# Attention and two experts on one core: reciprocal row sums spread by a GpSimd copy and five transposes instead of 64-column matmuls, and q/k transposes over all 128 rows

## The chip, the cores and the metric

The kernel runs on one core of one Trainium2 chip. The metric is the device time of one execution in microseconds; lower is better. The kernel uses five engines, each with its own instruction queue that is worked off in order: TensorE (PE, its weight loads shown as PEld), VectorE (DVE), ScalarE (ACT), GpSimd (POOL) and SyncE (SP), which issues the DMAs.

## What is computed

Attention over 2 batches and 8 heads of 576 rows and 64 columns, its output rearranged to 1152 tokens of 512, and two experts after it.

```python
def _attn_ref(q, k, v):
    ...
    q_rot, k_rot = (rotate(q), rotate(k))
    scale = 1.0 / np.sqrt(D)
    scores = scale * np.matmul(q_rot, k_rot.transpose(0, 1, 3, 2))
    scores = scores - np.max(scores, axis=-1, keepdims=True)
    attn = np.exp(scores)
    attn = attn / (np.sum(attn, axis=-1, keepdims=True) + 1e-09)
    return np.matmul(attn, v).astype(np.float32)

def reference(**kwargs):
    ...
    x = np.ascontiguousarray(attn_out.transpose(0, 2, 1, 3)).reshape(B * S, H * D)
    x = _moe_ref(x=x, **moe_kwargs)
    return _moe2_ref(x=x, **moe2_kwargs)
```

`_moe_ref` is `((x w_a) * (x w_b)) w_out` with 1536 inner columns, `_moe2_ref` is `(h - tanh(h)) w_out` with `h = x w_in` and 2048 inner columns.

## The kernel before

The attention works on eight pairs of heads, numbered 0 to 7. The 576 rows of a head are held as 64 rows by 9 chunks, two heads side by side: chunks 0 to 4 of a tensor stand on partitions 0 to 63 and chunks 5 to 8 on partitions 64 to 127, so that four columns of blocks (`c` = 0 to 3) fill 128 partitions and the fifth (`CM`, chunk 4) fills 64; its other 64 partitions were set to zero at the start.

For each pair the steps are:
- `load_qk`, `rope_step` (rope, on DVE for pair 1 and on POOL from pair 2 on, tiles `r2` and `ro`), `prep_T`: the rotated tensor is transposed by TensorE into `psp` (line 362), split by ACT and DVE into two parts and spread by DMA. Pair 0 goes through `rope_head` and `prep_head` (line 323) instead.
- `s_unit` (nine a pair): scores into `pss` (line 408, four matmuls), the negated maximum on DVE (line 414); `s_exp`: the exponential on ACT with the row sums in `sm` (line 420).
- `t_unit` and `t_tail`: the exponentials are transposed into `pst` (lines 473, 454, 459, 460), then split by ACT (478) and DVE (480) into `ph`.
- `v_head`: four accumulations over `ph` with v into `acc` (line 500), copied by ACT into `xe`; for pairs 0 to 6 one half goes by DMA into `xsum` (line 524) and POOL adds the other (line 525, two adds a pair); the last pair does it on DVE.
- `norm_sum`: 1 / (sum + 1e-9) into `rs`, 128 partitions by 9.
- `norm_pair`: the nine columns of `rs` have to stand along the free axis on 64 partitions each. A plain matmul with the column, broadcast to 64 columns, as the weights and the identity as the moving operand does it: eight of 128 columns into `rb` (line 557), two of 64 into `rt` (line 561), each into one half of the partitions. DVE multiplies `xsum` by `rb` (569) and `rt` (571), casts it to `xt` (577), and POOL subtracts for the low part (578).

`rb`, `rt`, `psp` and `pst` share the pool `ps_t`, tag `t`, with three buffers; `pss` has two. `norm_pair` already had a second way, with a tile `rd` in which `norm_sum` spreads `rs` to 128 columns for each of five blocks:

```python
rd = ap1.tile([P, 5, P], F32, tag="rd", name="rd")
fn = (nc.vector.tensor_copy, nc.gpsimd.tensor_copy, nc.scalar.copy)[RDP]
```

`ap1` has one buffer per tag. The number `RDP` in the table `CFG` chooses: 3 the matmuls, 1 the copy on POOL.

The order is set in two stages. A table of events places each step at a multiple of half a unit (nine units a pair): `at(g0 + NS, norm_sum, j)`, `at(t0 - 18 + NP, norm_pair, j)`, with `NS` 19 and `NP` 31, so that a pair's `norm_pair` comes ten units after its `norm_sum` and one unit after the `norm_sum` of the next pair. A scheduler then orders the instructions on each engine by priorities and by its own view of readiness and adds the waits. The expert stages follow: ACT and DVE convert the weights in pieces while TensorE multiplies (lines 190 and 843).

Of the kernel before, what the change touches and what calls it, by code (L numbers as in the profile page):

```python
# [29 lines left out]
def attention_moe_kernel(  # L30
# [184 lines left out]
    # ------------------------------------------------------------ attention  # L215
    with ExitStack() as actx:
# [703 lines left out]
```

## Time and profile before

| | us |
|---|---|
| median of 3 runs | 632.19 |
| lowest and highest | 631.37, 632.22 |
| span of the profiled execution | 632.1 |
| PE busy in it | 608.2 |
| DVE, ACT, POOL busy | 481.1, 348.4, 132.4 |

The profile is of one execution, whose span of 632.1 us agrees with the median. Busy time of PE contains the overlap of matmuls that follow each other: an instruction's own duration is longer than the distance to the next one's start. How long a step holds TensorE is therefore read from starts. A group of rows names the line, engine, operation, tile written and tiles read; in the timeline a row merges neighbours of one kind (x4), and square brackets show an idle time before it and who ended it. `128*64` is rows by columns of the array in use, `128x128` what is moved.

### The profile page before, as it was taken

What the parts mean: (1) busy time and instruction counts of PE and PEld (TensorE: products, weight loads), DVE (VectorE), ACT (ScalarE), POOL (GpSimd) and SP (SyncE); (2) the same over time, 40 slices, a digit from 0 to 9 for tenths busy, and PEclk for the clock granted to TensorE, in tenths of its full rate; (3) what the DMA queues carried; (4) which work ended last, traced back from release to release, by engine and by line L of the source; (5) the groups of instructions that cost most, each with busy time, mean ns of one, the idle gap of its engine ahead of it and who ended that gap; (6) DMA issues with size and microseconds to landing.
All of it is one profiled execution on the core that took longest, in us unless ns stands there. A gap on an engine that the chain in (4) does not pass through costs nothing.

```text
span 632.1 us, 9300 instructions
## 1 busy us (share of the span) xinstructions
PE 608.2 (96%) x3588; PEld 568.3 (90%) x3588; DVE 481.1 (76%) x646; ACT 348.4 (55%) x579; POOL 132.4 (21%) x121
## 2 busy tenths in 40 slices
PE   7789999999999999999999999998999999999997
PEld 6578988998889999999999999988988988998975
DVE  6868877778788988787757568694976698899572
ACT  2468877787774555533323133356966673585350
POOL 4565877773331000000000000091000000000000
PEclk7789999999999999999999999997999999999999
DMA  3466656753542555534203123320001121310014
GB/s 85 124 157 150 141 131 152 174 127 92 140 153 67 171 166 185 167 111 130 71 8 126 67 67 133 107 94 1 1 1 66 67 66 41 100 60 1 1 40 110
DMA packets 37771, 60.92 MB, mean 96 GB/s; under 512 B 4064, under 2 KB 22496, under 8 KB 37728
## 3 DMA queue, kind: packets, MB, share of 16 engines
q1 hardware_dynamic: 37728, 60.34, 33.3%
q8 instruction: 28, 0.46, 0.3%
q14 instruction: 15, 0.12, 0.1%
HBM read 43.06 MB, written 2.36 MB: 72 GB/s over the span
## 4 chain that ended last, share of the span: by engine, by line
PE 79%; DVE 6%; ACT 6%; POOL 3%; DMA 3%; issue 2%; SPq 1%; POOLq 0%; ACTq 0%; DVEq 0%
PE ab L190 24%; PE h L190 11%; PE o L843 10%; PE y L190 9%; PE acc L500 6%; PE pss L408 6%; PE pst L473 4%; POOL yt L736 3%; PE ow L843 3%; PE psp L362 2%; PE rb L557 2%; ACT st L127 1%; DMA st<-in_moe_w_in_dram 1%; DMA st<-in_moe_w_out_dram 1%; DVE nm L414 1%
## 5 line engine op out<-in xcount | busy, mean ns | idle before, releaser
L190 PE MATMUL ab<-xt,w 128*128 128x384 f32 x504 | 88.6, 334 | 0.5 <-ACT w L152 0.5
L190 PEld LDWEIGHTS ab<-xt,w 128*128 128x128 f32 x504 | 87.4, 188 | 0.8 <-ACT w L152 0.8
L843 PE MATMUL o<-wc,g 128*128 128x512 f32 x348 | 83.8, 392 | 0.4 <-ACT g L818 0.3
L843 PEld LDWEIGHTS o<-wc,g 128*128 128x128 f32 x348 | 64.7, 188 | 14.1 <-ACT g L818 1.3
L190 PE MATMUL y<-g,wc 128*128 128x384 f32 x432 | 76.5, 334 | 0.0
L190 PEld LDWEIGHTS y<-g,wc 128*128 128x128 f32 x432 | 75.0, 188 | 0.0
L408 PE MATMUL pss<-k,q 128*128 128x288 f32 x320 | 64.7, 323 | 2.4 <-ACT p L420 1.3
L414 DVE TENSOR_REDUCE nm<-pss 128x1 f32<-128x576 f32 x72 | 54.0, 753 | 15.9 <-PE pss L408 15.6
L190 PE MATMUL h<-yt,w 128*128 128x384 f32 x360 | 65.4, 335 | 0.1
L190 PEld LDWEIGHTS h<-yt,w 128*128 128x128 f32 x360 | 62.9, 188 | 1.7 <-issue 0.5
L736 POOL TENSOR_TENSOR yt<-yacc,yt 128x384 fp32r<-128x384 f32 x12 | 19.8, 1685 | 207.4 <-ACT yt L735 207.4
L190 PE MATMUL ab<-xt,wc 128*128 128x384 f32 x360 | 63.2, 334 | 0.0
L190 PEld LDWEIGHTS ab<-xt,wc 128*128 128x128 f32 x360 | 62.5, 188 | 0.0
L127 ACT ACTIVATE st<-st 128x1024 f32<-128x1024 f32 x34 | 39.9, 1172 | 35.5 <-DMA st<-in_moe_w_b_dram 16.2
L420 ACT ACTIVATE p<-pss,nm 128x576 f32<-128x576 f32 x72 | 54.0, 750 | 6.6 <-DVE nm L414 6.3
L500 PE MATMUL acc<-ph,v 128*128 128x288 f32 x320 | 55.4, 305 | 0.9 <-ACT ph L478 0.9
L408 PEld LDWEIGHTS pss<-k,q 128*128 128x128 f32 x320 | 47.5, 196 | 7.0 <-ACT p L420 4.3
L480 DVE TENSOR_TENSOR ph<-pst,ph 128x512 fp32r<-128x512 f32 x72 | 48.4, 684 | 4.8 <-ACT ph L478 4.6
L703 ACT COPY tmpa<-ab 128x384 f32<-128x384 f32 x36 | 17.2, 478 | 61.9 <-PE ab L190 61.7
L478 ACT CAST ph<-pst 128x512 fp32r<-128x512 f32 x72 | 42.4, 595 | 10.9 <-PE pst L473 9.5
L500 PEld LDWEIGHTS acc<-ph,v 128*128 128x128 f32 x320 | 45.1, 188 | 2.0 <-issue 1.5
L473 PE MATMUL pst<-ident,p 128*128 128x128 f32 x288 | 45.5, 276 | 1.0 <-DVE ph L480 1.0
(118 smaller groups left out, 1009.1 us busy)
## 6 DMA issues: line engine op xcount, KB each, us to landing
st<-in_moe_w_out_dram SPq DMA_DIRECT2D x14, 1024.0 KB, 4.9
st<-in_moe_w_in_dram SPq DMA_DIRECT2D x8, 1024.0 KB, 5.2
q<-th SPq DMA_DIRECT2D x28, 288.0 KB, 4.9
st<-in_moe_w_a_dram SPq DMA_DIRECT2D x12, 512.0 KB, 3.8
st<-in_moe_w_b_dram SPq DMA_DIRECT2D x12, 512.0 KB, 5.0
k<-th SPq DMA_DIRECT2D x28, 160.0 KB, 2.7
vr<-in_v_dram SPq DMA_DIRECT2D x16, 128.0 KB, 2.9
out_dram<-oacc SPq DMA_DIRECT2D x16, 128.0 KB, 2.4
```

The costliest lines, as they stand in the source:

```text
L127: nc.scalar.activation(out=xs.bitcast(F32), in_=xs.bitcast(F32), func=AF.Copy, scale=2.0 ** -112)
L190: nc.tensor.matmul(ps, w(a), x(c), start=start and n == 0, stop=stop and n == 2)
L408: nc.tensor.matmul(ph[:, a], st, k2[i][:, j, ko + a * HS:ko + (a + 1) * HS], start=(n == 0), stop=(n == len(mms) - 1),)
L414: nc.vector.tensor_reduce(out=nm[:, u:u + 1], in_=ph, axis=AX.XY, op=ALU.max, negate=True)
L420: nc.scalar.activation(out=po.rearrange("p (a x) -> p a x", a=2), in_=ph, func=AF.Exp, bias=nm, scale=1.0, accum_out=sm,)
L473: nc.tensor.transpose(ps[:, t * P:(t + 1) * P], p[:, t, o:o + P], ident)
L478: nc.scalar.copy(out=pu[:, 0, qm(i)], in_=ps)
L480: nc.vector.tensor_tensor(out=pu[:, 1, qm(i)], in0=ps, in1=pu[:, 0, qm(i)], op=ALU.subtract)
L500: nc.tensor.matmul(acc, st, pslot(i, u)[:, s, a * HS:(a + 1) * HS], start=(u == 8 and s == 0), stop=(u == full[-1] and s == 1),)
L703: nc.scalar.copy(out=a[:, t], in_=r[0])
L736: (nc.gpsimd if YLP > d else nc.vector).tensor_tensor(out=yl, in0=o, in1=yh, op=ALU.subtract)
L843: nc.tensor.matmul(ps, g[:, a, i * P:(i + 1) * P], wc[:, c, f % 2], start=(n == 0 and m == 0), stop=(n == GE - 1 and m == 2),)
```

## The change

Three things. `RDP` in `CFG` goes from 3 to 1, so `norm_sum` now copies `rs` on POOL into `rd` (512 columns and 128), and `norm_pair` transposes the five blocks of `rd` (four into `rb`, one into `rt`); the product with `rt` becomes two of 64 partitions. In `prep_T` the `CM` block is transposed over all 128 rows, and the next block overwrites the 64 columns too many or nothing reads them. In `prep_head` the same holds for the first head (`j` = 0). Four section comments and one on a formula go too. With the old way's branches gone the line numbers move: 408 becomes 409, 473 474, 500 501, 525 526, 557 554, 561 555, 362 363; 541 and 545 are the two copies.

```diff
@@ -320,7 +320,8 @@
             w = o = 448 * j
             for c in ((0, 1, 2, 3, CM), (CM, 0, 1, 2, 3))[j]:
                 x = 64 if c == CM else P
-                nc.tensor.transpose(ps[:, w:w + x], src[0:x, c], ident[0:x, 0:x])
+                r = x if j else P
+                nc.tensor.transpose(ps[:, w:w + r], src[0:r, c], ident[0:r, 0:r])
                 w += x
             ps = ps[:, o:w]
             if n == 1:
@@ -359,7 +360,7 @@
             for c in cols:
                 r = 64 if c == CM else P
                 with hp('pT'):
-                    nc.tensor.transpose(ps[:, w:w + r], src[0:r, c], ident[0:r, 0:r])
+                    nc.tensor.transpose(ps[:, w:w + P], src[:, c], ident)
                 w += r
             with hp('th'):
                 nc.scalar.activation(out=th[:, o:o + w], in_=ps[:, 0:w], func=AF.Copy, scale=sc)
@@ -549,30 +550,14 @@
             rd = rds.pop(i)
             rb = ps_t.tile([P, 512], F32, tag="t", name="rb")
             rt = ps_t.tile([P, 512], F32, tag="t", name="rt")
-            if RDP == 3:
-                for j in range(2):
-                    r = slice(64 * j, 64 * j + 64)
-                    for t in range(CM):
-                        u = 4 * j + t
-                        nc.tensor.matmul(
-                            rb[r, t * P:(t + 1) * P], rd[:, u:u + 1].to_broadcast([P, 64]), ident,
-                            start=True, stop=True,
-                        )
-                    nc.tensor.matmul(
-                        rt[r, 0:64], rd[:, 8:9].to_broadcast([P, 64]), ident[:, r], start=True, stop=True,
-                    )
-            else:
-                for t in range(CM):
-                    nc.tensor.transpose(rb[:, t * P:(t + 1) * P], rd[:, t], ident)
-                nc.tensor.transpose(rt[:, 0:P], rd[:, CM], ident)
+            for t in range(CM):
+                nc.tensor.transpose(rb[:, t * P:(t + 1) * P], rd[:, t], ident)
+            nc.tensor.transpose(rt[:, 0:P], rd[:, CM], ident)
             x = xs_t.pop(i)
             nc.vector.tensor_tensor(out=x[:, qm(i)], in0=x[:, qm(i)], in1=rb, op=ALU.mult)
-            if RDP == 3:
-                nc.vector.tensor_tensor(out=x[:, qt(i)], in0=x[:, qt(i)], in1=rt[:, 0:64], op=ALU.mult)
-            else:
-                for j in range(2):
-                    r = slice(64 * j, 64 * j + 64)
-                    nc.vector.tensor_tensor(out=x[r, qt(i)], in0=x[r, qt(i)], in1=rt[r, r], op=ALU.mult)
+            for j in range(2):
+                r = slice(64 * j, 64 * j + 64)
+                nc.vector.tensor_tensor(out=x[r, qt(i)], in0=x[r, qt(i)], in1=rt[r, r], op=ALU.mult)
             xh, xl = (t[:, hp, b * S:(b + 1) * S] for t in xt)
             (nc.scalar.copy, nc.gpsimd.tensor_copy, nc.vector.tensor_copy)[XHE](out=xh, in_=x)
             nc.gpsimd.tensor_tensor(out=xl, in0=x, in1=xh, op=ALU.subtract)
```

The scheduler's order moves with it. On POOL, where the two adds of pair 2 stand between the v preparation and the k rope of pair 6, the queue before:

```order
L290 TENSOR_TENSOR v_95<-vr,v_95 128x4x64 [waits PE_49,Activation_49,Pool_49]
L525 TENSOR_TENSOR xsum<-xe,xsum 64x576 [waits DMAHW5_49]
L525 TENSOR_TENSOR xsum<-xe,xsum 64x576 [waits DMAHW6_49,Pool_49]
L273 TENSOR_TENSOR r_1497<-rawk,rtab 128x10x32 [waits DMAHW7_49,DMAHW0_49,Pool_49]
L273 TENSOR_TENSOR r_1497<-rawk,rtab 128x10x32
L278 TENSOR_TENSOR ro<-rawk,rtab 128x640 [waits PE_49]
```

and now, the copies for pair 3 reading `rs`:

```order
L290 TENSOR_TENSOR v_95<-vr,v_95 128x4x64 [waits PE_49,Activation_49,Pool_49]
L526 TENSOR_TENSOR xsum<-xe,xsum 64x576 [waits DMAHW5_49]
L541 COPY rd<-rs 128x512 [waits PE_49]
L545 COPY rd<-rs 128x128
L526 TENSOR_TENSOR xsum<-xe,xsum 64x576 [waits DMAHW6_49,Pool_49]
L273 TENSOR_TENSOR r_1497<-rawk,rtab 128x10x32 [waits DMAHW7_49,DMAHW0_49,Pool_49]
L273 TENSOR_TENSOR r_1497<-rawk,rtab 128x10x32
```

The two adds stood together and the k rope followed at once. Now the copies of the next pair stand between them, and the first copy waits for PE, whose transposes of pair 2 read the one buffer of `rd`.

On PE, at the reciprocal step of pair 2, before:

```order
L408 MATMUL pss<-k_1044,q_93 128x288 x4
L557 MATMUL rb<-ident,rs 64x128 x2
L408 MATMUL pss<-k_1044,q_93 128x288 x4
L557 MATMUL rb<-ident,rs 64x128 x2
L561 MATMUL rt<-ident,rs 64x64
L557 MATMUL rb<-ident,rs 64x128 x4
L561 MATMUL rt<-ident,rs 64x64
L500 MATMUL acc<-ph,v_96 128x288
L362 MATMUL psp<-ident,ro 128x64
L362 MATMUL psp<-ident,ro 128x128 x3
L408 MATMUL pss<-k_1044,q_93 128x288 x4
```

and now:

```order
L409 MATMUL pss<-k_1045,q_93 128x288 x4
L554 MATMUL rb<-ident,rd 128x128 x2
L409 MATMUL pss<-k_1045,q_93 128x288 x4
L554 MATMUL rb<-ident,rd 128x128 x2
L555 MATMUL rt<-ident,rd 128x128
L501 MATMUL acc<-ph,v_96 128x288
L409 MATMUL pss<-k_1045,q_93 128x288 x4
L363 MATMUL psp<-ident,ro 128x128 x4
L501 MATMUL acc<-ph,v_96 128x288 x3
L474 MATMUL pst<-ident,p 128x128 x2
```

Ten matmuls of 64 output rows became five transposes, and the k transposes are all of one shape. Between `rt` and the next `pst` there are four `pss`, four `psp` and four `acc` matmuls.

## Rows read from the trace of the kernel before

**Rows 1.** The page: busy time by engine, and the chain by line.

```profile
PE 608.2 (96%) x3588; PEld 568.3 (90%) x3588; DVE 481.1 (76%) x646; ACT 348.4 (55%) x579; POOL 132.4 (21%) x121
PE ab L190 24%; PE h L190 11%; PE o L843 10%; PE y L190 9%; PE acc L500 6%; PE pss L408 6%; PE pst L473 4%; POOL yt L736 3%; PE ow L843 3%; PE psp L362 2%; PE rb L557 2%; ACT st L127 1%; DMA st<-in_moe_w_in_dram 1%; DMA st<-in_moe_w_out_dram 1%; DVE nm L414 1%
```

**Rows 2.** Stretches, one pair each: length, busy by engine, PEclk, DMA share, GB/s.

```profile
102.70:123.10 20.40, 20.11 (x154) 18.48 (x154) 16.03 (x31) 16.30 (x43) 15.30 (x16) 1.00 0.63 150
...
143.50:163.40 19.90, 19.49 (x150) 17.88 (x150) 15.56 (x30) 15.82 (x42) 6.75 (x8) 1.00 0.54 124
```

**Rows 3.** Chain of waits by line, in 62.2 to 143.5, 143.5 to 195, 20 to 62.2.

```profile
by line: PE acc L500 27.2%; PE pss L408 24.5%; PE pst L473 16.8%; PE psp L362 9.8%; PE rb L557 8.7%; DVE ph L447 2.8%; DVE nm L414 2.5%; ACT v L289 1.5%; ACT xe L522 1.5%; issue 1.1%; ACT ph L445 1.0%; PE rt L561 1.0%; PE pst L459 0.5%; PE 
...
by line: PE acc L500 26.4%; PE pss L408 16.8%; PE pst L473 14.2%; PE rb L557 13.3%; ACT p L420 4.6%; PE psp L362 3.9%; ACT st L127 2.3%; ACT w L152 2.2%; DVE st L135 2.2%; issue 2.2%; ACT ph L478 2.1%; PE ab L190 1.9%; DVE ph L447 1.7%; ACT
...
by line: PE pss L408 22.9%; PE acc L500 12.6%; PE pst L473 10.8%; PE psp L362 10.7%; DVE ro L280 8.4%; DVE nm L414 6.2%; ACT p L420 5.2%; DVE ph L480 4.5%; DVE rs L533 3.5%; ACT ph L478 2.8%; issue 2.0%; ACT th L365 1.8%; DVE q L339 1.8%; D
```

**Rows 4.** Groups of PE instructions: xcount | busy us, mean ns | idle before, releaser.

```profile
L473 PE MATMUL pst<-ident,p 128*128 128x128 f32 x288 | 45.5, 276 | 1.0 <-DVE ph L480 1.0
...
L557 PE MATMUL rb<-ident,rs 128*64 128x128 f32 x128 | 14.9, 280 | 2.5 <-DVE ph L447 1.6 <-DVE ph L480 0.9
...
L362 PE MATMUL psp<-ident,ro 64*128 64x64 f32 x28 | 7.8, 278 | 3.7 <-DVE ro L280 2.8 <-DVE ph L480 1.0
```

**Rows 5.** PE in order of time, 102 to 112: start us, us, instruction.

```profile
102.75 0.62 PE L557 MATMUL rb<-ident,rs 128*64 128x128 f32 x4 [0.38 <-DVE ph L447]
103.30 0.78 PE L408 MATMUL pss<-k,q 128*128 128x288 f32 x4
104.01 0.71 PE L557 MATMUL rb<-ident,rs 128*64 128x128 f32 x6
...
105.42 0.40 PE L500 MATMUL acc<-ph,v 128*128 128x288 f32 x1
105.75 0.75 PE L362 MATMUL psp<-ident,ro 64*128 64x64 f32 x4
106.25 0.77 PE L408 MATMUL pss<-k,q 128*128 128x288 f32 x4
106.86 0.70 PE L500 MATMUL acc<-ph,v 128*128 128x288 f32 x4
107.39 0.27 PE L473 MATMUL pst<-ident,p 128*128 128x128 f32 x1
...
110.20 1.06 PE L362 MATMUL psp<-ident,ro 64*128 64x64 f32 x6
111.19 0.67 PE L408 MATMUL pss<-k,q 128*128 128x288 f32 x3
```

**Rows 6.** PE in order of time, 187 to 190: eight full transposes.

```profile
187.21 1.04 PE L473 MATMUL pst<-ident,p 128*128 128x128 f32 x8
188.00 1.31 PE L500 MATMUL acc<-ph,v 128*128 128x288 f32 x8
```

**Rows 7.** Groups of POOL instructions: the nearest prices for a copy.

```profile
masks.py:199 POOL TENSOR_SCALAR_AFFINE_SELECT ident<-ident 128x128 f32<-128x128 f32 x1 | 0.3, 292 | 0.1
masks.py:197 POOL MEMSET ident<- 128x128 f32 x1 | 0.2, 205 | 0.3 <-POOLq L898 0.3
...
L898 POOL MEMSET const-float32-0.0<- 128x1 f32 x1 | 0.1, 98 | 0.2 <-issue 0.2
```

**Rows 8.** POOL in order of time, 102 to 124: its longest waits in one pair.

```profile
103.89 1.40 POOL L525 TENSOR_TENSOR xsum<-xe,xsum 64x576 f32<-64x576 f32 x1 [0.70 <-DMA xsum<-xe]
...
108.06 1.56 POOL L278 TENSOR_TENSOR ro<-rawk,rtab 128x640 f32<-128x640 f32 x1 [1.00 <-PE psp L362]
...
120.26 0.32 POOL L296 TENSOR_TENSOR v<-vt,v 64x64 fp32r<-64x64 f32 x1 [1.95 <-ACT v L295]
```

**Rows 9.** DVE in order of time, 122 to 129: the product and its wait.

```profile
125.89 0.69 DVE L569 TENSOR_TENSOR xsum<-xsum,rb 128x512 f32<-128x512 f32 x1 [0.41 <-PE rb L557]
126.49 0.21 DVE L571 TENSOR_TENSOR xsum<-xsum,rt 128x64 f32<-128x64 f32 x1
```

More of the change, by code (lines that the diff above doesn't have):

```diff
@@ L1 @@
-CFG = {'EXPF': 1, 'MAXF': 1, 'TT0': 20, 'TT1': 17.5, 'NS': 19, 'NP': 31, 'LK': -8, 'LQ': -2, 'RK': -2, 'RQ': 1, 'PK': 2, 'PQ': 4.5, 'LV': 7, 'PV': 9, 'WC1': 6, 'WC2': 4, 'PST': 3, 'RE': 2, 'FST': 0, 'CY': 1, 'CA': 2, 'CH': 2, 'OE': 3, 'VA0': 5.5, 'VA1': 7, 'VB0': 0, 'VB1': 2, 'PKD': 1, 'PQD': 0, 'PVD': 2, 'PVE': 0, 'XHE': 2, 'RST': 0, 'PA': 99, 'PB': 0, 'PO': 4, 'YLP': 4, 'GA': 0, 'GB': 0, 'WF': 99, 'WCE': 5, 'NH': 2, 'HA': 0, 'NT2': 2, 'RB': -50, 'SB': -49, 'NW': 20, 'NW1': 6, 'TM': 1, 'CO': 1, 'CHB': 0, 'WG': 99, 'WCG': 4, 'TL': 7, 'P_pl': 0, 'P_norm_sum': 30, 'P_load_v': 0, 'P_prep_v': 30, 'P_pT': 60, 'P_tl': -15, 'XL': 7, 'RDP': 3, 'P_ph': 0, 'P_exp': -60, 'P_V': 0, 'P_rope_head1': 0, 'P_load_qk': 15, 'P_S': 0, 'P_xs': -15, 'P_T': 0}
+CFG = {'EXPF': 1, 'MAXF': 1, 'TT0': 20, 'TT1': 17.5, 'NS': 19, 'NP': 31, 'LK': -8, 'LQ': -2, 'RK': -2, 'RQ': 1, 'PK': 2, 'PQ': 4.5, 'LV': 7, 'PV': 9, 'WC1': 6, 'WC2': 4, 'PST': 3, 'RE': 2, 'FST': 0, 'CY': 1, 'CA': 2, 'CH': 2, 'OE': 3, 'VA0': 5.5, 'VA1': 7, 'VB0': 0, 'VB1': 2, 'PKD': 1, 'PQD': 0, 'PVD': 2, 'PVE': 0, 'XHE': 2, 'RST': 0, 'PA': 99, 'PB': 0, 'PO': 4, 'YLP': 4, 'GA': 0, 'GB': 0, 'WF': 99, 'WCE': 5, 'NH': 2, 'HA': 0, 'NT2': 2, 'RB': -50, 'SB': -49, 'NW': 20, 'NW1': 6, 'TM': 1, 'CO': 1, 'CHB': 0, 'WG': 99, 'WCG': 4, 'TL': 7, 'P_pl': 0, 'P_norm_sum': 30, 'P_load_v': 0, 'P_prep_v': 30, 'P_pT': 60, 'P_tl': -15, 'XL': 7, 'RDP': 1, 'P_ph': 0, 'P_exp': -60, 'P_V': 0, 'P_rope_head1': 0, 'P_load_qk': 15, 'P_S': 0, 'P_xs': -15, 'P_T': 0}
 from contextlib import ExitStack, nullcontext
```

## The prediction

> **What bounds the kernel now.** I read the page's first and fourth parts, then the stretches pair by pair, then the chain of waits in three stretches, then the TensorE rows of one pair. The page says that PE is busy 96% of 632.1 us and heads the chain; lines 362 and 557, which the change touches, are 2% of it each [rows 1]. That is an average over two very different stages. Everything the change touches lies in the attention stage, which ends near 195 us. There one pair of heads, counted from one first `rb` to the next, takes 20.4 us and a later one 19.9. In the former PE is busy for 20.1 us, but DVE (16.0), ACT (16.3) and POOL (15.3) are not far behind, and after 143 us POOL falls to 6.75 because no rope is left [rows 2]. PE's granted clock is 1.00 in these stretches.
>
> A busy PE may still be a waiting PE, since matmuls overlap, so the chain decides. From 62.2 to 143.5 us the five PE lines it names first (500, 408, 473, 362, 557) carry 87% of it, and `rb` (8.7%), `rt` (1.0%) and `psp` (9.8%) together 19.5%. In 143.5 to 195 `rb` is 13.3% and `psp` 3.9%; in 20 to 62.2 `psp` is 10.7%, and DVE and ACT hold much of the rest [rows 3]. So four steady pairs are limited mainly by PE, and these two steps are a fifth of what limits them.
>
> **TensorE, reciprocal sums.** A plain matmul leaves two records, 128 of `rb` for its 64 matmuls over eight pairs, so a pair's ten leave twenty. A transpose leaves one: 288 records of line 473 for 8 x 9 x 4 transposes [rows 4]. In one pair the first four `rb` records hold PE from 102.75 to 103.30 (0.55 us), and the other twelve with four `rt` from 104.01 to 105.42 (1.41 us): 1.96 us [rows 5]. Eight full transposes take 187.21 to 188.00, so 0.099 us each [rows 6]. Five are 0.50 us. A pair saves 1.46 us.
>
> The Trainium skill (TensorEngine Tiling (Array Packing), Key Properties) says that tiles work independently and run in parallel, which speaks against this change: by it half-width matmuls would share the array, the twenty would be worth about 0.98 us, an estimate of half of what the rows show, and the saving a third of mine. The trace does not agree for these: sixteen records in 1.41 us are 0.09 us each, nearly a full transpose's 0.099.
>
> **TensorE, q/k transposes.** Each of seven pairs has two tensors of six transposes; the two 64-row ones become full ones. The q tensor's six hold PE from 110.20 to 111.19, 0.99 us, where six full ones are 0.59; the k tensor's first four hold it from 105.75 to 106.25, 0.50 us, where four are 0.40 [rows 5]. So changing the array's shape costs more than the extra rows. I take 0.4 us for q and 0.3 for k, whose last two also change shape once, plus an entry: one `acc` matmul before the first 64-row transpose takes 0.33 us (105.42 to 105.75), where four in a row take 0.53 (106.86 to 107.39) [rows 5], so 0.2 at an entry. About 1.1 us a pair with two entries.
>
> **PE sum, by the chain.** I count only what the chain holds. 62.2 to 143.5: 19.5% of 81.3 is 15.9 us; in its place stand four times 0.50 and 48 transposes at 0.099, 6.8 us; it saves 9.1. 143.5 to 195: `rb` and `psp` are 17.2% of 51.5, 8.9 us, against four times 0.50 and twelve transposes, 3.2; it saves 5.7. 20 to 62.2: `psp` is 4.5 us against 24 transposes, 2.4; it saves 2.1. Together 16.9 us. Per step without the chain it would be 8 x 1.46 + 7 x 1.1 = 19.4, the most I could defend. The first pair's `prep_head` also widens two transposes from 64 rows to 128; they stand beside DVE's rope and I cost them at nothing, at 2 x 0.099 us if that cover is gone.
>
> **POOL.** New are two copies a pair, 512 and 128 columns. No such broadcast copy is in the trace. From below: a memset takes 98 ns for one column and 205 for 128, 0.84 ns a column, so 0.73 us for the two. From above: the two-input add takes 1.40 us for 576 columns, so 1.56. I take the affine select, which reads one input and writes one output as a copy does: 292 ns for 128 columns, 1.53 ns a column, 1.17 us [rows 7]. That is 9.4 us of POOL over eight pairs. In the ropes' pairs POOL then has 15.3 + 1.2 = 16.5 us of work. In such a pair it is idle for 20.4 - 15.3 = 5.1 us, its longest waits 0.70, 1.00 and 1.95 us [rows 8], which the copy may fill.
>
> The Trainium skill (GPSIMD Engine Reference, section 4.1) has one-input work at roughly line rate. By the 1.03 cycles an element of its section 3.1 the copies would be some 0.55 us, an estimate; the sum below would gain about 1 us. No run here shows it.
>
> **The wait that takes the removed one's place.** `rd` has one buffer, so a pair's copy waits until the transposes of the pair before have read it. The order puts the copies of pairs 3 to 6 (of 0 to 7) between the two adds of the pair before. There the second add, then the DVE product and then the release of `rb` and `rt` all follow the transposes, and these two hold two of the three buffers of `ps_t`. Before, the product waited only for PE, 0.41 us, with both adds done [rows 8, 9]. Now from `rt` to the freed buffer it is 1.17 + 1.40 + 0.69 = 3.26 us. For pair 2 PE has between `rt` and its next `pst` one `acc`, four `pss`, four `psp`, three `acc`: eight matmuls at 0.13 and four transposes, 1.46 us, so about 1.8 us of waiting. For pair 3 it has four `psp`, eight `acc` and four `pss`: 2.0 us, so 1.3. For pair 4 the order has put 3 us of work there, and from pair 5 on no rope competes for the third buffer. I give back 3.1 us. Queued behind the product on DVE are the next maxima, and for those `pss` and ACT's exponentials.
>
> **DVE.** One 128x64 product of 0.21 us becomes two of 64x64, each no longer [rows 9]: 0.2 us a pair, beside 4 us of idle DVE time, at nothing. If DVE becomes the bound it costs 1.7 us in all.
>
> **Haircut and sum.** With a pair at some 18.1 us (20.4 less 9.1/4) DVE and ACT are 90% busy and POOL 91%, all in strict order, so short waits grow. I take a tenth of the saving, 1.7 us; that share is chosen, between nothing and the 8 us of the third case below. 632.1 - 16.9 + 3.1 + 1.7 = 620.0. The span is 632.1 us and the median of the three runs 632.19, so nothing is added. The expert stages have the same work in the same order; I leave them as they are. SP's queue gets no new transfer.
>
> **The rivals.**
> 1. Main case, 616.5 to 624: as above. Chance 0.50.
> 2. PE saving in full: the copy is as cheap as its lower bound, 0.73 us, and the third buffer comes free early. 632.1 - 16.9 = 615.2, 612.7 by the step count; taken as 612.5 to 616.5. For it speaks the chain, against it the 80% loads of DVE and ACT. Chance 0.14.
> 3. POOL or DVE takes over in the four rope pairs, which stay near 20.4 us, and only the 5.7 and 2.1 us outside them are won: 632.1 - 7.8 = 624.3; up to 629 if the tail, where ACT's and DVE's weight parts stand in the chain [rows 3], gives half of its 5.7 back and DVE's 1.7 come on top. For it: POOL's waits are ordered waits and may not be filled by the copy. Chance 0.23.
> 4. No change, within 0.2% (1.3 us, about what a measurement of this kernel can tell from none): PE merely waits where it worked. Against it: 87% of the chain is PE. Chance 0.05.
> 5. Slower: POOL's copy holds up the ropes. A rope pair is then POOL's own: 15.3 of work, 1.6 of copy, the 5.1 us of idle time kept, and 2 us, chosen, of waiting for the transposes: 24.0 us. Four such pairs add 14.4, less 7.8 elsewhere: 638.7. It decides once a rope pair goes above 20.4 + 7.8/4 = 22.4 us. Against it: PE's waits before `psp` name only ropes made on DVE, never POOL's [rows 4]. Chance 0.08.
>
> Could the change fail to do what it says? The order shows five transposes and no 64-row `psp` on PE, so no.
>
> **How the numbers follow.** Cases 1 to 3 are faster: 0.87; case 4 same: 0.05; case 5 slower: 0.08. The likeliest is case 1, 620.0. Its own range is 616.5 to 624. The range to give takes in most of case 2 and of case 3: 613 to 629; outside are cases 4 and 5 and thin ends, some 0.17.
>
> **What would show it.** Right: the profile after has 40 records of `rb` and `rt` in place of 160, all `psp` as 128x128, pairs of about 18 us between one `rb` and the next, a copy row on POOL near 0.9 us for 512 columns, and a `xsum` product that waits for POOL in pairs 2 and 3. Expert stages start some 12 us earlier and last as long. Wrong: pairs still of 20 us with PE idle before `pst` or `pss` (case 3 or 4), PE waiting for `ro` from POOL (case 5), or a lower PE clock in the attention stage, which would upset every price here.

## The result, and the profile after

The changed kernel takes 621.1 us (median of four, 619.34 to 626.83), the kernel before on the same chip 631.78 (628.22 to 632.22). The ratio is 0.986 (0.9818 to 0.9903), so the change wins about 9 us by it, with medians 10.7 apart; 620.0 was forecast, and the range of 613 to 629 holds the result. The total came out nearly as forecast. Where it came from did not, and most of this section is about that.

The page of the changed kernel: busy time by engine, the granted clock in 40 slices, the chain by engine and by line.

```profile
PE 587.5 (95%) x3468; PEld 551.8 (89%) x3468; DVE 486.0 (79%) x654; ACT 347.8 (56%) x579; POOL 133.1 (22%) x137
...
PEclk9999999999999999999999999999999999999999
...
PE 72%; DVE 10%; ACT 8%; POOL 3%; DMA 3%; issue 2%; SPq 0%; POOLq 0%; ACTq 0%; DVEq 0%
PE ab L190 23%; PE h L190 11%; PE o L828 11%; PE y L190 9%; PE pss L409 5%; PE acc L501 5%; PE pst L474 4%; PE ow L828 3%; POOL yt L721 2%; ACT p L421 2%; ACT ph L479 2%; PE psp L363 1%; ACT st L127 1%; POOL xsum L526 1%; DMA st<-in_moe_w_in_dram 1%
```

The chain by engine of the kernel before:

```profile
PE 79%; DVE 6%; ACT 6%; POOL 3%; DMA 3%; issue 2%; SPq 1%; POOLq 0%; ACTq 0%; DVEq 0%
```

Against [rows 1], PE is busy 20.7 us less, and its share of the chain has gone from 79% to 72%, to DVE and ACT; `rb` is gone from the list of lines and POOL's add, line 526, has come in. The span is 617.6 us, that execution's own time 619.34. So a time is some 1.8 us above its span, and the profiled execution of before, span 632.1, must have taken about 633.9.

I split each span at three marks that PE's rows give: the first `rb`, the first `y` matmul, the first `h` matmul. Each row below has a stretch, its length, then busy time and instructions of PE, PEld, DVE, ACT and POOL, then the granted clock, DMA share, GB/s. First the kernel before, in a view not shown ahead:

```profile
0.00:62.20 62.20, 50.23 (x289) 42.88 (x289) 46.64 (x94) 33.70 (x85) 32.74 (x35) 0.84 0.51 127
62.20:231.80 169.60, 165.98 (x1212) 155.63 (x1213) 138.72 (x233) 122.58 (x280) 79.90 (x75) 1.00 0.52 136
231.80:419.00 187.20, 187.20 (x1082) 187.20 (x1081) 135.27 (x172) 74.32 (x97) 9.66 (x7) 1.00 0.32 107
419.00:632.10 213.10, 204.81 (x1010) 182.55 (x1008) 160.50 (x150) 117.78 (x119) 10.13 (x6) 0.98 0.15 46
```

The same of the changed kernel:

```profile
0.00:54.90 54.90, 44.77 (x288) 38.83 (x289) 45.91 (x94) 33.48 (x85) 30.94 (x37) 1.00 0.57 143
54.90:222.00 167.10, 153.89 (x1094) 145.66 (x1093) 142.22 (x241) 121.73 (x279) 84.54 (x89) 1.00 0.52 138
222.00:409.20 187.20, 187.20 (x1082) 187.20 (x1081) 135.73 (x171) 74.19 (x95) 9.47 (x7) 1.00 0.32 107
409.20:617.60 208.40, 201.67 (x1010) 180.11 (x1008) 162.12 (x152) 118.38 (x120) 8.11 (x6) 1.00 0.16 47
```

The 14.5 us between these two spans are 7.3 before the first `rb`, 2.5 from there to `y`, none to `h`, and 4.7 after it. Two things are mixed in them. One is the clock: in the profiled execution of before PE ran at the lower level (1.2 GHz) for 20.5 us ahead of the first `rb` and for 6.8 near 430 us, in that of the change nowhere. These stretches differ between executions of one kernel, and the listed mean clocks show it: 0.977 to 0.993 for 23 executions of before on one chip, 0.984 to 1.000 for four of the change. So the clock is a rival for the whole gain. The times show how much of it: on that chip a straight line through time against listed mean clock falls by 0.32 us for each 0.001, both for the 23 of before and for six of the changed kernel (run e4 below, 0.978 to 0.999). At 0.985 the two lines read 631.1 and 624.6 us. By this estimate some 6.5 us of the gain stand at equal clock, and the other 2 or so come with the higher clocks that the changed kernel's executions had.

The other is the second row: PE's busy time fell by 12.1 us (165.98 to 153.89), but its idle time rose from 3.6 to 13.2 us, so 9.6 of the 12.1 were given back. That row is what the experiments are about.

Groups of the changed kernel: what the new work costs (xcount, then busy us and mean ns of one, then idle time before them and what ended it).

```profile
L363 PE MATMUL psp<-ident,ro 128*128 128x128 f32 x84 | 13.1, 276 | 0.8 <-DVE xsum L560 0.7
...
L562 DVE CAST xt<-xsum 128x576 fp32r<-128x576 f32 x8 | 5.9, 739 | 0.2
L554 PE MATMUL rb<-ident,rd 128*128 128x128 f32 x32 | 5.5, 274 | 0.8 <-DVE ph L481 0.4 <-DVE ph L448 0.4
L557 DVE TENSOR_TENSOR xsum<-xsum,rb 128x512 f32<-128x512 f32 x8 | 5.5, 685 | 4.4 <-POOL xsum L526 4.3
...
L541 POOL COPY rd<-rs 128x512 f32<-128x512 f32 x8 | 4.9, 613 | 9.2 <-PE rt L555 8.0 <-DVE rs L535 1.1
```

All 84 `psp` have the full shape, `rb` has 32 records. POOL waited 8.0 us for the transposes (`rt`) before copies, and DVE 4.3 us for POOL's add before products.

Now pair by pair, from one first `rb` to the next (columns as above), pairs 1, 2 and 3 of 0 to 7:

```profile
75.00:93.10 18.10, 17.46 (x139) 16.90 (x137) 15.36 (x31) 15.39 (x41) 16.07 (x17) 1.00 0.67 161
93.10:114.00 20.90, 18.19 (x136) 16.75 (x137) 17.10 (x32) 16.52 (x43) 18.67 (x20) 1.00 0.62 155
114.00:135.10 21.10, 18.06 (x140) 17.00 (x140) 17.11 (x31) 15.83 (x42) 15.04 (x16) 1.00 0.53 125
```

Pair 1 takes 18.1 us against 20.4 [rows 2], the length forecast for all four. Pairs 2 and 3, the two in which the prediction put the new wait, are longer than before. Pair 0, from 54.9 to 75.0 us, has won nothing either: 20.0 us, before 20.2. PE's waits in pair 2 (in total, times, longest):

```profile
PE pst L474 <- DVE xsum L557: 1.0, 1, 1.0
PE acc L501 <- ACT ph L479: 0.7, 1, 0.7
PE pst L474 <- DVE th L368: 0.6, 1, 0.6
PE rb L554 <- DVE ph L448: 0.4, 1, 0.4
PE pss L409 <- ACT p L421: 0.2, 1, 0.2
```

In pair 1 they are 0.3 us in all, here 2.9, and in pair 3 3.7: nearly the whole difference. POOL in order of time at the start of pair 2 (start us, us, instruction, idle before it):

```profile
92.08 1.42 POOL L526 TENSOR_TENSOR xsum<-xe,xsum 64x576 f32<-64x576 f32 x1
94.86 0.61 POOL L541 COPY rd<-rs 128x512 f32<-128x512 f32 x1 [1.36 <-PE rt L555]
95.41 0.30 POOL L545 COPY rd<-rs 128x128 f32<-128x128 f32 x1
95.79 1.40 POOL L526 TENSOR_TENSOR xsum<-xe,xsum 64x576 f32<-64x576 f32 x1
```

And DVE just behind:

```profile
97.22 0.69 DVE L557 TENSOR_TENSOR xsum<-xsum,rb 128x512 f32<-128x512 f32 x1 [1.25 <-POOL xsum L526]
```

The copy of the next pair stands between the two adds, is released by the transposes, and pushes the second add; the product is late, the bank it should free is late, and PE waits for it before `pst`. That is the mechanism as forecast. Behind it stands something that wasn't: the DVE cast of line 562 (577 before). The kernel before:

```profile
107.73 0.45 DVE L577 CAST xt<-xsum 128x576 fp32r<-128x576 f32 x1
```

In pair 3 of the changed kernel, on DVE:

```profile
120.02 1.78 DVE L562 CAST xt<-xsum 128x576 fp32r<-128x576 f32 x1
121.72 0.61 DVE L368 SCALAR_TENSOR_TENSOR th<-psp,th 128x448 fp32r<-128x448 f32 x1
```

and on POOL at the same time:

```profile
119.93 1.55 POOL L278 TENSOR_TENSOR ro<-rawk,rtab 128x640 f32<-128x640 f32 x1
```

A cast of 0.45 us lasts until 121.80, 0.3 us past the end of POOL's instruction, and `th`, for which PE's `pst` waits, stands behind it. In before the cast began at 107.73, ahead of POOL's rope at 108.06 [rows 8], and was not held: what holds it is the POOL instruction already running when it begins.

### The profile page after: what moved, and what is told of

Same layout as the page of the kernel before. It is cut to its first block, busy times and chain, and to the rows that moved or that the text cites. A ratio compares the mean times of both kernels' runs of the same rounds, so it can differ in the third digit from the quotient of the medians.

```text
span 617.6 us, 9091 instructions
## 1 busy us (share of the span) xinstructions
PE 587.5 (95%) x3468; PEld 551.8 (89%) x3468; DVE 486.0 (79%) x654; ACT 347.8 (56%) x579; POOL 133.1 (22%) x137
## 4 chain that ended last, share of the span: by engine, by line
PE 72%; DVE 10%; ACT 8%; POOL 3%; DMA 3%; issue 2%; SPq 0%; POOLq 0%; ACTq 0%; DVEq 0%
PE ab L190 23%; PE h L190 11%; PE o L828 11%; PE y L190 9%; PE pss L409 5%; PE acc L501 5%; PE pst L474 4%; PE ow L828 3%; POOL yt L721 2%; ACT p L421 2%; ACT ph L479 2%; PE psp L363 1%; ACT st L127 1%; POOL xsum L526 1%; DMA st<-in_moe_w_in_dram 1%
## 5 line engine op out<-in xcount | busy, mean ns | idle before, releaser
L409 PE MATMUL pss<-k,q 128*128 128x288 f32 x320 | 62.4, 315 | 6.6 <-ACT p L421 4.5
L415 DVE TENSOR_REDUCE nm<-pss 128x1 f32<-128x576 f32 x72 | 53.5, 752 | 11.2 <-PE pss L409 10.9
L721 POOL TENSOR_TENSOR yt<-yacc,yt 128x384 fp32r<-128x384 f32 x12 | 17.6, 1497 | 206.1 <-ACT yt L720 206.1
L501 PE MATMUL acc<-ph,v 128*128 128x288 f32 x320 | 56.8, 307 | 3.5 <-ACT ph L479 2.6
L409 PEld LDWEIGHTS pss<-k,q 128*128 128x128 f32 x320 | 45.8, 189 | 11.9 <-ACT p L421 9.0
```

The costliest lines, as they stand in the source:

```text
L409: nc.tensor.matmul(ph[:, a], st, k2[i][:, j, ko + a * HS:ko + (a + 1) * HS], start=(n == 0), stop=(n == len(mms) - 1),)
L415: nc.vector.tensor_reduce(out=nm[:, u:u + 1], in_=ph, axis=AX.XY, op=ALU.max, negate=True)
L501: nc.tensor.matmul(acc, st, pslot(i, u)[:, s, a * HS:(a + 1) * HS], start=(u == 8 and s == 0), stop=(u == full[-1] and s == 1),)
L721: (nc.gpsimd if YLP > d else nc.vector).tensor_tensor(out=yl, in0=o, in1=yh, op=ALU.subtract)
```

## The experiments

The table sums up the stretch from the first `rb` to the first `y` in each profile: its length, PE's busy and idle time in it, and the lengths of pairs 1, 2 and 3. The last column is the ratio to the kernel before on the same chip, over many executions each; it carries the verdicts. Pair lengths are taken from unrounded starts; in e7 3.4 us of the stretch ran at the lower clock. A pair is counted from its first `rb`, and a new order can move a step across that mark: the pairs shown hold 40 score matmuls (`pss`) each, but 36 in pair 2 of after, e3 and e4, and 44 in pair 3 of e1 and e7. Four of them are 0.6 us of PE [rows 5], so the stretch is the safer column.

| kernel | length | PE busy | PE idle | pairs 1, 2, 3 | ratio (95%) |
|---|---|---|---|---|---|
| before | 169.6 | 166.0 | 3.6 | 20.4, 20.4, 20.4 | 1 |
| after | 167.1 | 153.9 | 13.2 | 18.2, 20.9, 21.0 | 0.986 (0.982 to 0.990) |
| e1 transposes only | 172.4 | 164.1 | 8.3 | 22.3, 21.8, 21.9 | 0.9988 (0.996 to 1.0015) |
| e2 copy only | 171.3 | 157.8 | 13.5 | 21.2, 21.0, 21.5 | 1.0016 (0.9988 to 1.0044) |
| e3 change, two `rd` | 163.1 | 153.1 | 10.0 | 19.3, 18.9, 19.7 | 0.9842 (0.9815 to 0.9869) |
| e4 change again | 167.8 | 154.3 | 13.5 | 18.8, 20.9, 21.0 | 0.989 (0.9852 to 0.9927) |
| e5 e1, cast on ACT | 173.5 | 166.1 | 7.4 | 21.4, 21.3, 21.2 | 1.0024 (0.9989 to 1.0058) |
| e6 e3, cast on ACT | 161.8 | 152.5 | 9.3 | 20.0, 18.6, 17.9 | 0.982 (0.978 to 0.986) |
| e7 before, cast on ACT | 175.1 | 169.7 | 5.4 | 20.6, 21.4, 21.2 | 1.008 (1.005 to 1.0111) |
| e8 e3, more warming | 165.0 | 153.8 | 11.2 | 19.1, 20.6, 20.4 | 0.9899 (0.986 to 0.9939) |
| e9 change, no cast | 172.8 | 157.9 | 14.9 | 20.8, 21.0, 20.9 | 0.9965 (0.9939 to 0.999) |
| e10 e3, no cast | 167.4 | 155.9 | 11.5 | 20.5, 18.8, 20.6 | 0.9885 (0.9847 to 0.9922) |
| e11 e1, no cast | 170.9 | 164.6 | 6.3 | 20.9, 20.2, 21.1 | 0.9956 (0.9927 to 0.9986) |
| e12 e2, two `rd` | 168.5 | 157.9 | 10.6 | 19.8, 19.8, 21.0 | 0.9921 (0.9891 to 0.995) |

**The parts alone: e1, e2, and the change again, e4.** e1 has the wide q/k transposes and keeps the old reciprocal sums; e2 the reverse; e4 is the changed kernel.

e1, against the changed kernel:

```diff
-    'RDP': 1,
+    'RDP': 3,
...
+                        nc.tensor.matmul(
+                            rb[r, t * P:(t + 1) * P], rd[:, u:u + 1].to_broadcast([P, 64]), ident,
+                            start=True, stop=True,
+                        )
```

e2, against the changed kernel:

```diff
-                r = x if j else P
-                nc.tensor.transpose(ps[:, w:w + r], src[0:r, c], ident[0:r, 0:r])
+                nc.tensor.transpose(ps[:, w:w + x], src[0:x, c], ident[0:x, 0:x])
...
-                    nc.tensor.transpose(ps[:, w:w + P], src[:, c], ident)
+                    nc.tensor.transpose(ps[:, w:w + r], src[0:r, c], ident[0:r, 0:r])
```

> Only the q/k transposes read all 128 rows; the reciprocal sums stay with the 64-column matmuls, so POOL has no copy. Theory A (the new wait of the POOL copy on PE ate most of what PE won in the rope pairs) and theory B (what PE saves passes through) agree here: rope pairs of 20.4 - 0.8 to 1.1 = 19.3 to 19.6 us from one rb to the next, about 6 us in all, near 626 us. Theory C (most of the difference between the two profiles is TensorE's clock in the first 46 us and near 425 us, which falls to half in some executions and not in others, whatever the kernel): the time goes with the listed clock, near 617 at 1.000 and near 628 at 0.978, and an execution at 1.000 has its first rb some 7 us earlier than one at 0.978.

> Only the POOL copy and the five transposes; q/k transposes of the fifth block stay at 64 rows. Theory B: 10.8 us of the PE sum, near 621, pairs of 18.9 us. Theory A: the copy of a pair stands between the two adds of the pair before and waits for its transposes, so rope pairs stay at 20.4 to 21.5 us, and the whole gains 0 to 4 us, 628 to 632. Theory C: 7 to 12 us between executions at clock 1.000 and 0.978.

> The changed kernel itself, again, for the times against the listed clock. Theory C: its executions spread over 619 to 627 and go with the clock, about 0.4 to 0.5 us for each 0.001 of mean clock; with no half-clock stretch near 617 to 620. If instead the clock of the first 46 us is the change's doing, all executions stand at 0.99 or above and the kernel before at 0.98.

Measured: 629.73 us (e1), 631.71 (e2) and 622.86 (e4), against 631.28 for before. Neither part alone can be told from no change, and together they win 7 to 9 us. The time does go with the listed clock, as theory C had it (by 0.32 us for each 0.001, where it expected 0.4 to 0.5), but at like clock e4 stays ahead of before and e1 does not: at 0.997 e4 took 620.40 and e1 629.06 us, at 0.993 before took 628.72. The table shows why the parts are no contradiction of the PE prices: in e2 PE is busy 8.2 us less and idle 9.9 us more, in e1 1.9 less and 4.7 more. In e1 the waits of the stretch 75 to 147 us include these:

```profile
POOL ro L278 <- PE psp L363: 6.8, 3, 2.7
...
PE pst L474 <- DVE th L368: 3.1, 3, 1.0
```

So cheaper transposes alone move which engine waits: the rope on POOL waits for `psp`, 1.9 to 2.7 us in each of pairs 1 to 3 (before 1.0 to 1.7), the cast there (1.71 to 1.72 us) is held beside POOL, and PE waits for `th`. And e1 has one more price, on PE itself, in pair 2:

```profile
99.03 0.87 PE L558 MATMUL rb<-ident,rs 128*64 128x128 f32 x6
...
99.94 0.66 PE L363 MATMUL psp<-ident,ro 128*128 128x128 f32 x4
100.53 1.09 PE L558 MATMUL rb<-ident,rs 128*64 128x128 f32 x8
...
101.66 0.54 PE L501 MATMUL acc<-ph,v 128*128 128x288 f32 x2
```

The order puts the k transposes between the two halves of the old sums, which hold PE 0.91 and 1.13 us here and, with their first two records (97.41 to 97.78), 2.41 in all, where they held it 1.96 in before. Counted from start to next start, or to an instruction's own end if that comes first, over the whole stretch, the transposes hold PE 3.1 us less in e1 (9.5 to 6.5) and the sums 1.4 more (15.2 to 16.5). So e1 is not the transposes' price alone.

**The copy's wait: e3 and e12.** Two `rd` buffers, so that a copy waits for no transpose:

```diff
-            rd = ap1.tile([P, 5, P], F32, tag="rd", name="rd")
+            rd = ap2.tile([P, 5, P], F32, tag="rd", name="rd")
```

> The changed kernel with two buffers for rd, so that a copy does not wait for the transposes of the pair before; in its order the copies stand ahead of both adds. Theory A: the 20.9 and 21.0 us pairs fall to 18 to 18.6, the rows of the product no longer show a wait for POOL of over 1 us, and the time is 4 to 7 us under the changed kernel's, near 615. Theory B: no wait mattered, same as the changed kernel within 2 us.

> The copy and the five transposes alone (e2), with two rd buffers, so that POOL's copy does not wait for the transposes of the pair before. Theory (in e2 the shorter PE work is there, but the copy's wait, 4.0 us in three pairs, and the late add, product and cast behind it give it back): rope pairs of 19 to 20 us in place of 21.0 to 21.5, first rb to first y 165 to 168 in place of 171.3, ratio 0.988 to 0.994. Rival (the 1.46 us a pair that the sums cost PE were covered by other engines anyway, and only both parts together bring PE under them): rope pairs stay at 20.4 or more, ratio 0.997 to 1.003.

e3 measured 620.42 us (619.12 to 622.21) beside 622.86 for e4 on the same chip. POOL in e3 at the place of the four rows above has both adds in one run, no copy and no wait between them:

```profile
96.27 2.90 POOL L526 TENSOR_TENSOR xsum<-xe,xsum 64x576 f32<-64x576 f32 x2
```

PE's waits in its pair 2 have lost those for `xsum` and `th`:

```profile
PE acc L501 <- ACT ph L479: 0.7, 1, 0.7
PE rb L554 <- DVE ph L448: 0.4, 1, 0.4
PE pss L409 <- ACT p L421: 0.3, 1, 0.3
```

The stretch is 4.7 us shorter than in e4, with PE's work 1.2 us less, so 3.5 of it is idle time. In the times the gain over e4 is 2.4 us, and the intervals of the two ratios overlap; so in the changed kernel itself a gain by the second buffer is likely, not shown. e12 is the clearer pair: the copy alone goes from 1.0016 with one buffer to 0.9921 (626.67 us) with two, and the intervals lie apart. The ratio came in as the first theory expected; the stretch, 168.5 us, missed its 165 to 168 by a little, and of the pairs two were 19.8 us and the third, with a held cast of 1.77 us, 21.0. The rival, that PE's saving on the sums was covered anyway, falls. The one buffer costs about 6 us where the copy stands alone.

**The held cast: e5, e6, e7, then e9, e10, e11.** First the cast goes to ACT:

```diff
-    'XHE': 2,
+    'XHE': 0,
```

> The q/k transposes of the change alone, as in e1, with the cast of the finished pair to its first float32r part moved from DVE to ACT. Theory (the cast on DVE is held while a POOL instruction runs: 0.45 us in the kernel before, 1.72 us in e1, and th, then PE's pst, stand behind it): the cast costs ACT about 0.55 us and nothing waits for POOL, so the four rope pairs of e1 (22.3, 21.8 and 21.9 us for the three that stood out) fall to 20.5 or less, the stretch from the first rb to the first y falls from 172.4 to at most 169, and the ratio is 0.991 to 0.995. Rival (POOL's own work and its waits for psp set these pairs, the long cast only fills time that is waited anyway): pairs stay at 21.5 or more, ratio 0.997 to 1.001.

> The change with two rd buffers (e3) and the cast on ACT. Theory of the held cast: the rope pairs fall from 18.9 to 19.7 us to about 18.5, first rb to first y from 163.1 to about 160, time 2 to 3 us under e3, ratio 0.980 (0.977 to 0.982). Rival (ACT, busy for 16.3 of 20.4 us before, becomes the late engine): no gain over e3, ratio 0.984 to 0.988.

> The kernel before with the cast on ACT alone. There the cast fell into POOL's own wait for PE and took 0.45 us, so the theory of the held cast expects next to nothing: ratio 0.999 to 1.002, stretch from first rb to first y 169 to 171. Rival (the cast on DVE costs time whether or not it is held): ratio 0.993 to 0.997, the same gain as in the other two.

Measured: 633.37, 618.5 and 635.61 us against 630.83. On ACT the cast takes 0.66 to 0.69 us and is never held, but e5 wins nothing, as the rival had it: against e1 its pairs 1 and 2 are 1.4 us shorter together, and its pairs 3 and 4 are 1.9 us longer. The kernel before loses 0.8% by the same edit, which neither of my theories had. Part of that is on PE: the new order splits the sums again, and over the stretch they hold PE 17.3 us in e7, in e5 as well, where before has 15.2. That is 2.1 of the 5.5 us by which e7's stretch is longer. For the rest, ACT, too, works in order, and the cast and a wait for the product now stand between its exponentials; that this is the cause is likely, but no run isolates it. e6 is the fastest kernel of the study, yet its interval takes in e3's ratio, so whether the cast's move helps there stays open.

Then the cast is replaced by a second product into the float32r part:

```diff
+            nc.vector.tensor_tensor(out=xh[:, qm(i)], in0=x[:, qm(i)], in1=rb, op=ALU.mult)
             nc.vector.tensor_tensor(out=x[:, qm(i)], in0=x[:, qm(i)], in1=rb, op=ALU.mult)
...
-            (nc.scalar.copy, nc.gpsimd.tensor_copy, nc.vector.tensor_copy)[XHE](out=xh, in_=x)
```

> The change, with the cast of the finished pair taken away: the first float32r part is written by a second product of xsum with rb and rt, straight from PSUM, so DVE does 1.12 us of product (0.685 and two of 0.216) where it did a cast of 0.45 us, or of 1.1 to 1.8 us beside POOL. Theory (DVE's cast, and of DVE's instructions hardly any other, is held until POOL's instruction ends, and the rope pairs with a held cast are the long ones: 18.2 us with 0.46, 20.9 with 1.11, 21.0 with 1.79): products are not held, so the second product lasts 1.12 us in every pair, the four rope pairs come to 18.2 to 19.2 us, the stretch from the first rb to the first y falls from 167.1 to 161 to 164, and the ratio is 0.977 to 0.983. Rival (the long cast only fills time in which PE waits for something else): rope pairs stay at 20.5 or more, ratio 0.986 to 0.992.

> As e9, with two rd buffers as in e3. Theory of the held cast: in e3 two of the three rope pairs held casts of 1.85 and 1.79 us; now rope pairs of 18 to 18.8 us, first rb to first y 159 to 162 in place of 163.1, ratio 0.976 to 0.982. If it is the wait of the copy alone that costs time: no gain over e3, ratio 0.984 to 0.988.

> The q/k transposes alone (e1), with the cast replaced by a second product in the same way. Theory of the held cast: e1's three long rope pairs (22.3, 21.8, 21.9 us, with casts of 1.71 to 1.72) come down to 19.3 to 20.2 (its pairs with a free cast, 18.7 to 19.3, and 0.67 of longer product), the stretch from the first rb to the first y from 172.4 to 165 to 168, ratio 0.988 to 0.994. Rival (POOL's ropes and their waits for psp set these pairs): they stay at 21 or more as in e5, ratio 0.998 to 1.004.

Measured: 631.01, 625.1 and 629.62 us against 632.29. The products are not held (0.67 to 0.69 us in every pair), yet e9 is slower than the change, with intervals apart, and e10 no faster than e3. The forecast of the theory of the held cast, pairs of about 18 us, fails in both. The edit does not test the hold by itself, though, since it also adds a second product. The chain of waits of e9 in its pair 2 shows where the new price stands:

```profile
101.60 0.06 POOL rd L541
...
102.15 0.30 POOL rd L545
...
102.53 1.43 POOL xsum L526
...
103.98 0.69 DVE xt L558
...
104.79 0.60 DVE xsum L559
...
105.42 0.22 DVE xt L562
```

The second product lies on the very chain that the late copy makes: from the add to the freed bank it is now one product longer, in each pair, while a held cast was longer in two or three. In e10, with two buffers, no copy waits for the transposes and no cast is held, and yet pairs 1 and 3 take 20.5 and 20.6 us; PE waits there for ACT's `ph` and `p` and for the second product, 1.9 us a pair. So these two waits are not the whole reason for long pairs. Only in e11, with no copy and no wait, does the edit help: 0.9956 against 0.9988 for e1, with overlapping intervals. So the hold is a fact of the traces; that time can be won by avoiding it is not shown.

**The clock: e8.** 24 warming transposes in place of 6 at each of four places ahead of the pairs, on top of e3:

```diff
-    'NW1': 6,
+    'NW1': 24,
```

> The change with two rd buffers (e3) and 24 instead of 6 warming transposes after each head's preparation of the first pair. Theory (the mean clock of an execution, 0.977 to 1.000, differs by half-clock stretches before the first rb, where PE is often idle, and those shift the whole time by up to 8 us): granted clock 1.00 up to the first rb, mean clock 0.995 or more in most executions, first rb at 55 to 57 us in place of 57.8, times closer together, ratio 0.979 to 0.983. Rival (the stretches come whatever PE does there, and the warming only adds 72 transposes to it): mean clocks as spread as in e3, ratio 0.985 to 0.990.

The granted clock was 1.00 up to the first `rb`, the mean clock of six executions 0.995 to 1.000 (e3: 0.983 to 0.989), and the times lie within 623.31 to 625.43. So with more warming the lower level is no longer seen there, as the theory had it. The time came out as its rival had it: the first `rb` comes at 60.2 us (57.8 in e3, forecast 55 to 57), pairs 2 and 3 take 20.6 and 20.4, and the time is 623.78. Pair 2 has 0.6 us of `pss` more than e3's, and in both pairs PE waits 1.1 us for `th`, behind casts of 1.57 us, and 0.7 for the product. Why the order came out so with nothing but warming added, I leave open.

## Why the prediction was right in the sum and not in its terms

**PE's prices** held in detail. PE of the changed kernel in order of time, in pair 2:

```profile
93.13 0.41 PE L554 MATMUL rb<-ident,rd 128*128 128x128 f32 x2 [0.37 <-DVE ph L448]
93.67 0.80 PE L409 MATMUL pss<-k,q 128*128 128x288 f32 x4
94.30 0.38 PE L554 MATMUL rb<-ident,rd 128*128 128x128 f32 x2
94.52 0.27 PE L555 MATMUL rt<-ident,rd 128*128 128x128 f32 x1
...
96.00 0.63 PE L363 MATMUL psp<-ident,ro 128*128 128x128 f32 x4
96.39 0.64 PE L501 MATMUL acc<-ph,v 128*128 128x288 f32 x3
...
101.38 0.84 PE L363 MATMUL psp<-ident,ro 128*128 128x128 f32 x6
101.98 0.78 PE L409 MATMUL pss<-k,q 128*128 128x288 f32 x4
```

Six full q transposes of the changed kernel hold PE from 101.38 to 101.98 us, 0.60 (forecast 0.59); four of k from 96.00 to 96.39, 0.39 (0.40). In the stretch from the first `rb` to `y` the two chain terms, 9.1 and 5.7, promised 14.8 us. Counted from starts, as the prediction counts, the sums fell from 15.2 to 4.7 us, 1.3 a pair where I had 1.46, and `psp` from 9.5 to 5.7: 14.3 together. PE's busy time fell by only 12.1, because its other matmuls, `acc` and `pst` above all, hold it 2.2 us longer than before. The five transposes are cheap one by one (two in 0.22 us at 94.30), but the first two, with the start of the `pss` behind them, hold PE for 0.54 us.

**What the prediction read wrongly on PE** is why ten narrow matmuls cost so much. It set the rule of the Trainium skill (TensorEngine Tiling (Array Packing), Key Properties), that tiles run in parallel, against the average of 0.09 us a record, and found that the trace did not agree. Record by record it does agree. The old loop sends five matmuls to one half of the columns and then five to the other, and within a half records start 0.109 us apart. Only where the two runs meet do neighbours use different halves, and there they run side by side: in pair 2 of before, records of the first half start at 104.28, 104.39 and 104.50 us and those of the second at 104.29, 104.45 and 104.55. Where e1's order parts the halves, no such overlap is left, and the sums cost 2.41 us instead of 1.96. Whether a loop that alternates between the halves would have made the old sums cheap, without any copy, no run here tests.

**The copy** costs 0.613 and 0.297 us, 0.91 a pair; I took 1.17, between 0.73 and 1.56. By the GPSIMD Engine Reference, section 3.1, of the Trainium skill it would be 0.55, an estimate; the trace does not agree in the sum. It does in the rate: the estimate is 0.86 ns a column, and from 128 to 512 columns the copies differ by 0.82 ns a column; each has some 0.19 us besides. Of the signs, "near 0.9 us for 512 columns" did not come: that copy takes 0.61.

**The step that failed is the give-back**: "The wait that takes the removed one's place" at 3.1 us, with the "Haircut" of 1.7, 4.8 together. PE's idle time in the stretch grew by 9.6 us. The place and the chain were right (copy between the adds, late product, bank not free, in pairs 2 and 3), but I priced only the wait for the bank, 1.8 and 1.3 us; it came to 1.0 and 1.3. What I left out is what else is queued behind the late product on DVE: the cast, `th` and the maxima, and behind them PE's `pst` and ACT's `ph`; so 2.9 and 3.7 us of PE's waits stand in those pairs in place of 0.6 or less. "From pair 5 on" and pair 4 I priced at nothing, and the tail's 5.7 us of saving did not come either: pairs 4 and 5 took 20.0 and 19.7 us, before 19.9 and 20.1, and 19.1 and 17.9 with two buffers. By pairs the 9.6 us are 1.3 in pair 0, 0.3 in pair 1, 2.4 and 2.7 in pairs 2 and 3, 1.2 and 0.4 in pairs 4 and 5 and 1.3 after them. So only half of it stands where the forecast wait stands. In pair 0 PE waits for ACT's `ph` and `p` and DVE's `ph` (0.8, 0.5 and 0.4 us), and in e3 the same, so that part is not the one buffer's; what makes ACT and DVE late there no run isolates. **DVE at nothing** was wrong in the same way: the product's two halves are 0.216 us each and harmless, but the cast, an instruction the change doesn't touch, grew from 3.6 us in eight to 5.9, by the company it got on POOL.

**What made up for it** lies outside the chain that I summed. Before the first `rb` I had 2.1 us; the profiles show 7.3. Executions with the wide transposes and the granted clock that before had there (0.84) come to the first `rb` at 58.4 us (e6, 0.82) and 59.5 (e9, 0.83) in place of 62.2, so about 3 of the 7.3 are the change's and some 4 the clock's. That split is rough: without the wide transposes e12 came to it at 59.3 (0.86) and e2 at 63.6 (0.89). After `h` nothing was forecast, and the 4.7 us there have the same work: PE is busy 3.1 us longer in before, with half of 6.8 us at the lower clock level to answer for it, and it waits 3.2 us for `yt` against 1.8. Without the clock that leaves 2.5, about 3 and about 1.4 us, near the 6.5 estimated at equal clock and about half of the 12.1 forecast. So 621 beside 620.0 is partly luck: the give-back was twice as large as forecast, and shares that I had priced lower or not at all, the clock's among them, filled the gap.

**The base.** I took the profiled span, 632.1, for that execution's time; it lacks 1.8 us. So the sum stood against an execution above the median by 1.7, and the forecast saving of 12.1 us compares with 8.8 (by the ratio; 6 to 11.5 by its interval).

**The rivals.** Pair 1 went the way of the main case, pairs 2 and 3 that of the third, where DVE and POOL take over. The fifth, ropes that hold up PE, did not come: PE's waits in the stretch name no `ro`. The second, the full saving, is not reached even with two buffers. Of the signs of being right these came: 40 records of `rb` and `rt`, all `psp` in the full shape, and a product that waits for POOL; pairs of 18 us came only once, and the expert stages 9.8 us earlier, not 12. Of the signs of being wrong, PE idle before `pst` in pairs over 20 us came too.

Still open: whether the change itself keeps the clock up more often in the first 50 us. Its executions show it (e4: 0.978 to 0.999, before on the same chip 0.977 to 0.993), but so few cannot settle it.

## What to carry to other kernels

When an engine is 98% busy in a stage and the others 75 to 80%, a saving on it is worth only what the others have free in order: here 12 us of work on PE became 2.5 us in that stretch. A step moved to an in-order engine should be read with what stands on both sides of it: one more buffer for the new tile, one word of code, is worth trying first: it was worth 6 us to the copy alone, and a likely 2 or 3 to the whole change. Before a step is moved off an engine, read it record by record: the average of 0.09 us hid that the same ten narrow matmuls cost 1.96 us in one order and 2.41 in another. Judge parts together as well as apart, since two that gain nothing alone gained 7 to 9 us together, and compare the granted clock of two profiles stage by stage before explaining the difference of their spans.

## What was not expected of the hardware

- The DVE cast from float32 to float32r, 128x576 in SBUF, takes 0.45 us when no POOL instruction is running at its start. Where one was, the cast ended 0.31 to 0.32 us after that instruction if this came later than its own 0.45: with 0.08 us of it left the cast took 0.46 in pair 1 of the changed kernel, with more left 0.73, 1.11 and 1.78 in pairs 0, 2 and 3, and up to 1.85 in e3. Of DVE's other instructions the like happened to single-input scalar operations (128x9 of `rs`, 0.16 us: 1.45 us once in before, 1.74 in e9) and to one with two inputs in SBUF (a 128x1024 weight piece, line 154, 1.23 us: 2.39 once in e1), never to the products with a PSUM input (0.685 us). The Trainium skill (VectorE: DVE Perf Modes, "The perf-mode tier table") lists copies and scalar operations on float32 in SBUF at double rate and a two-input product with a PSUM input at single rate, and the GPSIMD Engine Reference, section 1, has the SBUF interfaces shared with VectorE, with contention in its 2-port modes or with two SBUF inputs. The traces agree in what is held and what is not, with these numbers.
- Where these profiles show the lower clock level (1.2 GHz) before the last 4 us of a span, it stood ahead of the first `rb`, between 415 and 440 us, or once near 185, in lengths that differed between executions: 0 to 20.5 us ahead of the first `rb`.
- Narrow matmuls (64 of 128 columns) overlap where neighbours use different halves: records of two halves start within 6 ns of each other at the halves' border in pair 2 of before (104.28 and 104.29), and 0.109 us apart inside a half.
- Each of the six kernels with the cast moved or replaced differs from its fellow by an edit of about 1 us a pair or less, and their pairs range from 17.9 to 21.4 us: with four engines over 70% busy, each in strict order, I could not forecast a pair's length from the prices of its parts.
